# Strassen products of float32 replaced, from the second token block on, by three float32r passes over 12-bit operand parts

## Chip, core and metric

One core of one Trainium2 chip. The metric is the time of one execution of the program on the device in microseconds (us), from its own clock; lower is better. A profile of one execution is taken by the hardware profiler. Engines: PE (TensorE, matmul; PEld is its weight load), DVE (VectorE), ACT (ScalarE), POOL (GpSimd), SP (SyncE, which issues the DMAs here).

## The reference

Two parts, one after the other. First a retention recurrence over 4 x 8 heads, 768 steps and head size 64; then, on its output read as 3,072 tokens of 512 values, a two-layer network with an ELU between.

```python
for t in range(S):
    state = gamma[None, :, None, None] * state + np.einsum('bhd,bhe->bhde', k[:, :, t], v[:, :, t])
    y[:, :, t] = scale * np.einsum('bhd,bhde->bhe', q[:, :, t], state)
...
h = x @ w_in
g = np.where(h > 0.0, h, alpha * (np.exp(np.minimum(h, 0.0)) - 1.0))
return (g @ w_out).astype(np.float32)
```

x is 3,072 x 512, w_in 512 x 2,048, w_out 2,048 x 512, all float32. Both weight matrices reach the device as 64-bit floats and are decoded there.

## The kernel before

Tokens go in six blocks of 512. The retention of a block is worked in four chunks of 128 tokens: score products (L319) masked by DVE (L330), state products (L359) summed by DVE (L371), outputs (L415, L430) scaled by DVE into `xb` or `xt` (L405). It is cut into five steps (`retention_step`), which are put between the matmuls of the block before.

Block 0 is worked while the weights arrive. A weight piece (1,024 columns of 64-bit floats, 1 MB) is loaded into one of three `stage` tiles, prepared by three ACT instructions (L171, L173, L175) and decoded by two of DVE (L198, L201). Layer 1 of block 0 uses plain float32 matmuls (`plain_first`, L518 and L542), four of 512 columns for each of 16 groups of 128 hidden values. Layer 2 of block 0 (`second_of_first`, L632) is one level of Strassen: seven products in place of eight on quarters, with sums of the weight pieces (`sums_of_pieces`, L582) and of the hidden values (`inputs_of_first`, L561) made by DVE, and closing sums at L616.

From block 1 on: while block 0 runs its layer 2, DVE forms the combinations of weights that later Strassen levels need (`combine_w_out` L668, `combine_w_in` L695, `combine_small` L852), and SP stores them to scratch memory on the device. Block 1 has one level of Strassen in layer 1 (`first`, L765) and two levels in layer 2 (`second_twice`, L924). Blocks 2 and 3 are taken together, as are 4 and 5 (`NB` = 2 rounds): layer 1 has two levels for the products that can have them (`big_twice`, L1152) and one for the rest (`big_rest`, L1199); layer 2 has two levels, 7 x 7 products of four matmuls (`second_big`, L1248). A product ends in PSUM; ACT lifts it (L1163, L1256) or DVE adds it to another (L1167, L1260), and further DVE sums make the inputs of the next product (`quarters_of`, L894; `next_big_input`, L1230). ELU is two ACT instructions (L1214, L1215) and one of DVE (L1216).

The order of work on each engine is the order of the program text: nothing is rescheduled. Python generators are stepped by hand so that, for example, a retention step stands between two products. Every engine, and the queue of SP, works its instructions in that order, and an instruction that waits holds up all behind it on its engine. Weights for the later products come from scratch memory through a ring of tiles (`wq`): `want` lists them in order of use, and `fetch` (L830) issues a load when `done` has released a tile. The chunks of q, k and v (1 MB each, four tiles in `ldpool`) come through the same SP queue (L113), and so do the stores of results.

PSUM has eight banks: four in pool `ps_r` (retention, and some accumulators of block 0) and `a`, `a`, `b`, `d` in `ps_f`, handed out by `bank`.

Of the kernel before, what the change touches and what calls it, by code (L numbers as in the profile page):

```python
# [10 lines left out]
FP32 = mybir.dt.float32  # L11
I32 = mybir.dt.int32
# [3 lines left out]
ALU = mybir.AluOpType  # L16


@with_exitstack
def kernel(  # L20
# [4 lines left out]
    scratch: bass.AP,  # L25
    scratch2: bass.AP,
    scratch3: bass.AP,
    scratch4: bass.AP,
# [3 lines left out]

# [14 lines left out]
    NQ = 4  # L68
    NF = DFF // P // 2
# [9 lines left out]
    mpool = mid.enter_context(tc.tile_pool(name="mpool", bufs=4))  # L79
    hpool = mid.enter_context(tc.tile_pool(name="hpool", bufs=4))  # L80
    small = mid.enter_context(tc.tile_pool(name="small", bufs=6))
# [3 lines left out]

    early = ctx.enter_context(ExitStack())
    stage = early.enter_context(tc.tile_pool(name="stage", bufs=3, side="right"))
    t4 = early.enter_context(tc.tile_pool(name="t4", bufs=1, side="right"))
    so_ = t4.tile([P, 2, 7, 256], FP32, name="so")


    gnames = ["C11", "C12", "C21", "C22", "T3"]
    gq = {x: const.tile([P, DFF // P // 2, TH], FP32, name="g" + x) for x in gnames}
    gq["T1"] = gq["C12"]
    four = lambda x: gq[x].rearrange("p (i a) t -> p i (a t)", a=2)
    g_plain = [four(x)[:, i, :] for x in gnames[:4] for i in range(4)]

# [17 lines left out]
    def hold(t, other):  # L115
# [4 lines left out]

    w_all = const.tile([P, NQ, 14 * TH], FP32, name="w_all")
    w_a_, w_b_, w_x_ = (
        w_all[:, :, 1024 * g : 1024 * g + 1024].rearrange("p n (f c k d) -> p n f c k d", f=2, c=2, k=2) for g in range(3)
    )
    w_y_ = w_all[:, :, 3072:3584].rearrange("p n (f k d) -> p n f k d", f=2, k=2)
    w_a, w_b, w_x, w_y = ([x[:, n] for n in range(NQ)] for x in (w_a_, w_b_, w_x_, w_y_))
    s_of = lambda n: (w_y[n], w_x[n][:, :, 0], w_x[n][:, :, 1])
    NPIECE = 2 * NQ + NF  # L130
# [20 lines left out]

    def prepare(parts=1, by_vector=False, between=None):
# [5 lines left out]
        if n < 2 * NQ:  # L160
            dst = (w_a, w_b)[n % 2][n // 2].rearrange("p a b c d -> p (a b c d)")
        else:

            dst = w_x[n % NQ].rearrange("p a b c d -> p (a b c d)")
        todo = []
        for part in range(parts):
            if part and between:
                between()
            c = slice(part * 1024 // parts, (part + 1) * 1024 // parts)
            lo, hi, flat = t[:, c, 0], t[:, c, 1], dst.bitcast(U32)[:, c]  # L170
            nc.scalar.activation(flat, lo, AF.Copy, scale=2.0**-29)  # L171
            top = dst.bitcast(F8).rearrange("p (c b) -> p c b", b=4)[:, c, 3]
            nc.scalar.activation(top, hi.bitcast(FP32), AF.Copy, scale=2.0**-120, saturate=False)  # L173
            if not by_vector:
                nc.scalar.activation(lo.bitcast(FP32), hi.bitcast(FP32), AF.Copy, scale=2.0**-112)  # L175
            todo.append((lo, flat, hi if by_vector else None))
        prepared.append((dst, todo))


    ORDER_F = [f for n in range(NF // 2) for f in (n, NF // 2 + n)]  # L180


    quarters = lambda f: scratch.rearrange("(s k) p (f c) -> k f p s c", k=2, f=4)[f // 4, f % 4]

    used = lambda f, a, b: slice(a, b, 2 if f < NF // 2 else 1)

    def decode(fine=False):
# [7 lines left out]
        for c, flat, hi in todo:  # L195
            if hi is not None:
                vec.tensor_scalar(c.bitcast(FP32), hi.bitcast(FP32), 2.0**-112, None, ALU.mult)
            vec.tensor_scalar(c, c, 3, 0x7FFFFFF8, ALU.logical_shift_left, ALU.bitwise_and)  # L198
            if fine:
                yield  # L200
            vec.tensor_tensor(out=flat, in0=c, in1=flat, op=ALU.add)  # L201
            yield
        load_piece()
        if n >= 2 * NQ:
            f = ORDER_F[n - 2 * NQ]
            nc.sync.dma_start(quarters(f)[:, used(f, 2, 8)], dst.rearrange("p (s c) -> p s c", c=P)[:, used(f, 2, 8)])
# [4 lines left out]

# [23 lines left out]
    nc.vector.tensor_scalar(vf, vf, scale, None, ALU.mult)  # L237
# [36 lines left out]

    xb = const.tile([P, 4, TB], FP32, name="xb")
    xt_ = const.tile([P, 4, 2, TH], FP32, name="xt")
    xt = [xt_[:, n] for n in range(4)]

    x_of = lambda tb: xb if tb in (0, 3, 5) else xt_.rearrange("p j a t -> p j (a t)")

    xt1 = [xb[:, n].rearrange("p (a t) -> p a t", a=2) for n in (1, 2, 3, 0)]
# [15 lines left out]
    def state(tb, n):  # L299
# [3 lines left out]
        if (tb, n) == (0, 3):  # L303

            return xt[0].rearrange("p a t -> p (a t)")[:, 0:256].rearrange("p (h e) -> p h e", e=D)
# [168 lines left out]
    def combine_x_parts(tb=None):  # L474
        sub = lambda o, x, y: nc.vector.tensor_tensor(out=o, in0=x, in1=y, op=ALU.subtract)
        b11, b12, b21, b22 = (x_of(tb)[:, 2 * r : 2 * r + 2, half[t]] for r in range(2) for t in range(2))
        t1, t2, t3, t4_ = xt1 if tb == 1 else xt
        sub(t1, b12, b11)
        yield
        sub(t2, b22, t1)  # L480
        yield
        sub(t3, b22, b12)
        yield
        sub(t4_, b21, t2)

# [7 lines left out]
    def elu(g, h, depth=1, then=None):  # L493


        r = epool.tile([P, 512], FP32, name="r", tag="r", bufs=3)
        e = r if len(h.shape) == 2 else r.rearrange("p (a c) -> p a c", c=P)
# [3 lines left out]
        def last():  # L501
            nc.vector.scalar_tensor_tensor(g, e, -1.0, h, ALU.add, ALU.max)
            if then:
                then()
# [5 lines left out]
    def plain_first():  # L510

        tiles = [(n, w, row, fi) for n in range(NQ) for w, row in ((w_a, 0), (w_b, 1)) for fi in range(2)]
        banks = []

        def part(k, columns):
            n, w, row, fi = tiles[k]
            for j in range(4):
                nc.tensor.matmul(  # L518
                    banks[k][:, columns], lhsT=w[n][:, fi, j // 2, j % 2, :], rhs=xb[:, j, columns],
# [14 lines left out]
        for k in range(5):  # L534
            part(k, half[1])
            n, w, row, fi = tiles[k]
            elu(g_plain[row * NF + 2 * n + fi], banks[k])
            yield
        for k, (n, w, row, fi) in enumerate(tiles[5:]):
            hp = bank("aabd"[k % 4]).rearrange("p a b -> p (a b)")  # L540
            for j in range(4):
                nc.tensor.matmul(  # L542
                    hp, lhsT=w[n][:, fi, j // 2, j % 2, :], rhs=xb[:, j, :], start=(j == 0), stop=(j == 3)
                )
            elu(g_plain[row * NF + 2 * n + fi], hp)
# [3 lines left out]
    def of_first(r, f, t, count=2):  # L549

        i = (r * NF + f) % 4
        g = gq[gnames[(r * NF + f) // 4]]
# [23 lines left out]
    def sums_of_pieces(n):  # L576
# [3 lines left out]
        both = w_all[:, n % NQ : n % NQ + 2, 2048:3072]  # L580
# [15 lines left out]
        for x in range(2):  # L596
            f = ORDER_F[n + x]
            of = sums[n + x].rearrange("p a (d c) -> p (a d) c", c=P)
            nc.sync.dma_start(quarters(f)[:, used(f, 8, 16)], of[:, used(f, 0, 8)])

    def small_of_pieces(at):

        sources = [
            (decoded[2 * NQ + n].rearrange("p r (d c) -> p (r d) c", d=2)[:, 1:4], sums[n])
            for n in (2 * at, 2 * at + 1)
        ]
        return combine_w_out(at, *sources)

    def second_of_first():
# [8 lines left out]
        def store(k):  # L618
            nc.sync.dma_start(out[0, k // 2, k % 2].rearrange("p d c -> p (d c)"), out_t[k].rearrange("p a b -> p (a b)"))

        for n, f in enumerate(ORDER_F):
            wo, so, x = decoded[2 * NQ + n], sums[n], inputs[f]
            a21, a11, a12, a22 = (wo[:, r, 256 * d : 256 * d + 256] for r in range(2) for d in range(2))
            w = {1: a11, 2: a12, 3: so[:, 0], 4: a22, 5: so[:, 1], 6: so[:, 2], 7: so[:, 3]}
            at_end = n == NF - 1
            if at_end:
                m1, u2, v, u3 = (mpool.tile([P, 2, TH], FP32, name="m", tag="m") for _ in range(4))
# [29 lines left out]


    SEVEN = {1: 0, 2: 1, 4: 2, 3: 3, 5: 4, 6: 5, 7: 6}
    to_send = []  # L660

    def send_small():
        while to_send:
# [1225 lines left out]
```

## Time and profile before

| | |
|---|---|
| runs | 620.98, 623.10 (median), 625.47 us |
| profiled execution: span of its instructions | 621.4 us |
| PE's first matmul, and end of its last | 1.5 us, about 618.4 us |
| block 0 ends, block 1's first product starts | 134.75 us |
| PE, DVE, ACT, POOL busy | 611.4, 496.7, 261.0, 21.2 us |
| DMA moved | 125.14 MB, 201 GB/s mean |
| granted PE clock | 1.000 throughout |

No own time of the profiled execution stands beside its span; the first instruction to the last is what the page measures, and the median of the three runs is 1.7 us more. Reading the page: a group's row gives the engine, the operation, `out<-in` by tile names, the shape, the count, then its busy time and the mean of one in nanoseconds, then the idle time of the engine before them and who ended it. Matmul ends are modelled, so the distance between starts is the better measure of a matmul. One float32 matmul leaves two records in the trace.

### The profile page before, as it was taken

To read this page: it belongs to the slowest core of one execution; us is meant where nothing else is said; L and a number is where in the kernel's file an instruction comes from. 1 tells how busy PE (TensorE), PEld (TensorE's weight loads), DVE (VectorE), ACT (ScalarE), POOL (GpSimd) and SP (SyncE) were. 2 spreads that over 40 slices of the span, in tenths; PEclk is the share of its full clock that TensorE was granted. 3 is DMA by queue.
4 is the path that set the end of the run, shared out by engine and by line. 5 is a ranking of instruction groups with operands and counts; after the bars stand their busy time and mean duration, and the time that the engine had idled before them with its cause. 6 is when DMAs were issued, how large, how long until landed. Compare 5 with 4: busy or idle time off the path is not lost.

```text
span 621.4 us, 13415 instructions
## 1 busy us (share of the span) xinstructions
PE 611.4 (98%) x5446; PEld 480.9 (77%) x5446; DVE 496.7 (80%) x776; ACT 261.0 (42%) x446; POOL 21.2 (3%) x30
## 2 busy tenths in 40 slices
PE   8999999999999999999999999999999999999998
PEld 6764568888889998888545888888888744788886
DVE  5768889989889875677888987898546897888885
ACT  5888844205542111236898210100144798511110
POOL 2011000000000001000010000110000000000000
PEclk9999999999999999999999999999999999999999
DMA  8697569789575898786811445873654523356453
GB/s 295 285 374 303 174 205 269 235 242 274 204 234 151 301 374 310 231 250 199 274 49 67 122 134 154 268 275 108 206 159 143 151 69 93 118 148 187 153 150 117
DMA packets 79278, 125.14 MB, mean 201 GB/s; under 512 B 6128, under 2 KB 46832, under 8 KB 74480
## 3 DMA queue, kind: packets, MB, share of 16 engines
q1 hardware_dynamic: 79216, 124.28, 62.1%
q8 instruction: 43, 0.70, 0.4%
q14 instruction: 19, 0.16, 0.1%
HBM read 94.63 MB, written 29.62 MB: 200 GB/s over the span
## 4 chain that ended last, share of the span: by engine, by line
PE 86%; DVE 4%; DMA 3%; ACT 3%; issue 2%; SPq 0%; DVEq 0%
PE pa L1248 15%; PE pa L1152 9%; PE pd L1248 8%; PE pa L1199 6%; PE pd L1152 4%; PE pa L765 4%; PE pd L1199 4%; PE pb L1248 4%; PE x L632 3%; DMA wq<-scratch_dram 2%; PE pa L924 2%; PE pa L542 2%; PE pb L1152 2%; PE pa L632 2%; PE pb L1199 2%; PE y L415 2%
## 5 line engine op out<-in xcount | busy, mean ns | idle before, releaser
L1256 ACT COPY ms<-pa 128x256 f32<-128x256 f32 x41 | 15.3, 372 | 108.5 <-PE pa L1248 105.5
L1248 PE MATMUL pa<-gC,wq 128*128 128x256 f32 x224 | 53.1, 381 | 0.0
L1248 PEld LDWEIGHTS pa<-gC,wq 128*128 128x128 f32 x224 | 42.1, 190 | 6.8 <-DVE gT L1216 0.5
L1215 ACT ACTIVATE r<-r 128x512 f32<-128x512 f32 x64 | 40.3, 630 | 2.0
L1163 ACT COPY m<-pa 128x512 f32<-128x512 f32 x32 | 18.7, 585 | 48.9 <-PE pa L1152 48.8
L293 POOL TENSOR_TENSOR chunk<-chunk,vf 128x512 f32<-128x512 f32 x16 | 18.0, 1124 | 381.3 <-DMA chunk<-in_qkv_dram 201.1
L1260 DVE TENSOR_TENSOR res<-pd,ms 128x256 f32<-128x256 f32 x26 | 11.0, 422 | 25.0 <-PE pd L1248 14.1
L1152 PE MATMUL pa<-ts,wq 128*128 128x256 f32 x104 | 26.9, 384 | 0.0
L1248 PE MATMUL pa<-ts,wq 128*128 128x256 f32 x112 | 26.8, 382 | 0.0
L1248 PE MATMUL pd<-w_all,wq 128*128 128x256 f32 x112 | 26.6, 380 | 0.1
L171 ACT ACTIVATE w_all<-wraw 128x1024 uint32<-128x1024 uint32 (+1 forms) x19 | 19.2, 1008 | 16.9 <-PE x L632 9.0
L1248 PE MATMUL pd<-ts,wq 128*128 128x256 f32 x104 | 24.7, 380 | 0.2 <-DVE ts L894 0.2
L1230 DVE TENSOR_TENSOR gC<-w_all,gC 128x1024 f32<-128x1024 f32 x20 | 24.2, 1260 | 0.0
L1248 PEld LDWEIGHTS pd<-w_all,wq 128*128 128x128 f32 x112 | 21.2, 190 | 3.4 <-DVE w_all L894 0.6
L1248 PEld LDWEIGHTS pa<-ts,wq 128*128 128x128 f32 x112 | 21.0, 190 | 2.9
L1248 PE MATMUL pa<-w_all,wq 128*128 128x256 f32 x96 | 22.9, 381 | 0.0
L173 ACT ACTIVATE w_all<-wraw 128x1024 fp8e4<-128x1024 f32 (+1 forms) x19 | 22.6, 1189 | 0.6
L1152 PEld LDWEIGHTS pa<-ts,wq 128*128 128x128 f32 x104 | 19.3, 190 | 4.5 <-ACT m L1163 0.8
L1216 DVE SCALAR_TENSOR_TENSOR w_all<-r,w_all 128x512 f32<-128x512 f32 x32 | 22.0, 688 | 0.7 <-ACT r L1215 0.6
L1248 PEld LDWEIGHTS pd<-ts,wq 128*128 128x128 f32 x104 | 19.7, 190 | 3.2 <-DVE ts L894 0.6
L1199 PE MATMUL pa<-ts,wq 128*128 128x512 f32 x48 | 22.1, 592 | 0.0
L1199 PE MATMUL pa<-gC,w_all 128*128 128x512 f32 x48 | 22.1, 592 | 0.0
(327 smaller groups left out, 1458.0 us busy)
## 6 DMA issues: line engine op xcount, KB each, us to landing
wq<-scratch_dram SPq DMA_DIRECT2D x191, 256.0 KB, 3.2
chunk<-in_qkv_dram SPq DMA_DIRECT2D x22, 1024.0 KB, 7.6
wraw<-in_w_dram SPq DMA_DIRECT2D x15, 1024.0 KB, 7.1
out_dram<-res SPq DMA_DIRECT2D x7, 512.0 KB, 3.3
scratch_dram<-gT SPq DMA_DIRECT2D x12, 256.0 KB, 4.3
wq<-scratch_dram SPq DMA_DIRECT2D x24, 128.0 KB, 3.1
scratch_dram<-w_all SPq DMA_DIRECT2D x12, 256.0 KB, 3.4
scratch_dram<-w_all SPq DMA_DIRECT2D x24, 128.0 KB, 3.2
```

Of the source, the lines that this page charges most:

```text
L171: nc.scalar.activation(flat, lo, AF.Copy, scale=2.0**-29)
L173: nc.scalar.activation(top, hi.bitcast(FP32), AF.Copy, scale=2.0**-120, saturate=False)
L293: eng.tensor_tensor(out=v, in0=v, in1=vf[:, i].unsqueeze(2).to_broadcast([C, H, D]), op=ALU.mult)
L632: nc.tensor.matmul(X[j][:, d, :], lhsT=w[j][:, d * P : d * P + P], rhs=x[j], start=(n == 0 and d == 0), stop=at_end, skip_group_check=True,)
L765: nc.tensor.matmul(ps[:, fi, :], lhsT=w[:, fi, j2, :], rhs=x[:, j2, :], start=(begin and fi == 0 and j2 == 0), stop=(j2 == 1), skip_group_ ...
L1152: nc.tensor.matmul(ps[:, f, :], lhsT=w[:, f, :], rhs=big_xs[j][k], start=(begin and f == 0), stop=True, skip_group_check=True,)
L1163: nc.scalar.copy(o, ps)
L1199: nc.tensor.matmul(ps, lhsT=w[:, k, :], rhs=layer_x[j][:, k], start=False, stop=(k == 1), skip_group_check=True,)
L1215: nc.scalar.activation(r, r, AF.Exp, scale=-1.0)
L1216: return lambda: nc.vector.scalar_tensor_tensor(g, r, -1.0, g, ALU.add, ALU.max)
L1230: nc.vector.tensor_tensor(out=quarter(to, r, t), in0=quarter(x, r, t), in1=quarter(y, r, t), op=op)
L1248: nc.tensor.matmul(ps, lhsT=w[:, f, :], rhs=ts[j][k][:, f // 2, f % 2, :], start=(begin and f == 0), stop=(f == 3), skip_group_check=True,)
```

## The change

Block 0 keeps its products. From block 1 on there is no Strassen: each float32 operand is cut into a high part and a low part of 12 bits, of type float32r, and a product is made of three passes accumulated in PSUM: high x high and low x low, then the bank is multiplied by 1 + 2^-12 (`scaled`), then a third pass with the differences of the parts on both sides. Five blocks of 512 tokens follow, each with 16 groups of 12 passes in layer 1 and 16 groups of 12 passes in layer 2, all with 512 columns.

- Weights of layer 2: `parts_of_w_out` cuts each decoded piece into three parts (one ACT copy, two DVE instructions of 1,024 columns) in one tile, and stores them to scratch in three DMAs of 512 KB. It is called eight times, from the 13th step of layer 1 of block 0 to the end of its layer 2.
- Weights of layer 1: `parts_of_w_in` cuts each of 16 tiles (ACT copy, DVE low part, POOL difference) and stores high and low part; the first two are made at the end of block 0, the others inside layer 1 of block 1. In later blocks high and low come back by DMA, and POOL makes the difference (`third_of_w_in`).
- Activations: `split_x` cuts the input of a block, `split_g` each of 16 groups of hidden values (ACT copy, DVE low part, difference by DVE or, for odd groups, POOL).
- The high part of w_out stays on chip (`wo1`); its low part and difference are loaded again for each block, through a ring of eight tiles.
- Retention of the next block now stands inside layer 1 of each block, the chunk loads (`load`) and `scale_v` of the block after that inside layer 2.
- All combinations of weights, inputs and products of the later Strassen levels go, with their scratch memory.

The core of the diff (removed: `combine_x_parts`, `combine_w_out`, `combine_w_in`, `strassen`, `first`, `second_twice`, `big_twice`, `big_rest`, `second_big` and what they call):

```diff
+    def stt(o, a, by, b, op):
+        nc.vector.scalar_tensor_tensor(o, a, by, b, ALU.mult, op)
+
+    def parts_of_w_out(n):
+        t = w_parts.tile([P, 3, 2, DM], F32R, name="wp", tag="wp")
+        piece, (hi, lo, d) = flat(w_x_[:, n % NQ]), (flat(t[:, x]) for x in range(3))
+        nc.scalar.activation(hi, piece, AF.Copy, scale=W_PART * CUT)
+        stt(lo, piece, W_PART, hi, ALU.subtract)
+        stt(d, hi, R, lo, ALU.subtract)
+        f = ORDER_F[n]
+        for x in range(3):
+            nc.sync.dma_start(s_out[x, f : f + NP + 1 : NP].rearrange("f p c -> p f c"), t[:, x].bitcast(FP32))
...
+    def split_g(tb, f, by_pool=False):
...
+        nc.scalar.activation(g_hi[f], g, AF.Copy, scale=R * CUT)
+        stt(g_lo[f], g_hi[f], -1.0 / R, g, ALU.add)
+        (nc.gpsimd if by_pool else nc.vector).tensor_tensor(out=g_d[f], in0=g_lo[f], in1=g_hi[f], op=ALU.subtract)
...
+    def split_x(tb, i):
+        x, (hi, lo, d) = x_of(tb)[:, 2 * i : 2 * i + 2], (xp[:, n, 2 * i : 2 * i + 2] for n in range(3))
+        nc.scalar.activation(hi, x, AF.Copy, scale=CUT * PART / X_DOWN)
+        stt(lo, x, PART / X_DOWN, hi, ALU.subtract)
+        stt(d, hi, R, lo, ALU.subtract)
...
+    def fetch(count=1):
+        for _ in range(count):
+            if wanted:
+                name, source = wanted.popleft()
+                got[name] = ring.tile([P, TB], F32R, name="w", tag="w")
+                nc.sync.dma_start(got[name].bitcast(FP32), source)
...
+    def parts_of_w_in(f, tiles):
+        hi, lo, d = got[1, 0, f], got[1, 1, f], got[1, 2, f] = tiles
+        w = w_of(f).rearrange("p k c -> p (k c)")
+        nc.scalar.activation(hi, w, AF.Copy, scale=R * CUT)
+        stt(lo, hi, -1.0 / R, w, ALU.add)
+        nc.gpsimd.tensor_tensor(out=d, in0=lo, in1=hi, op=ALU.subtract)
+        for n, t in enumerate((hi, lo)):
+            nc.sync.dma_start(s_in[n, f], t.bitcast(FP32))
...
+    def first_two(tb, f):
+        hp = flat(ps_r.tile([P, 2, TH], FP32, name="hp", tag="r") if f < 2 else bank("aabd"[(f - 2) % 4]))
+        banks1[f] = hp
+        for n in range(2):
+            for k in range(NK):
+                one_pass(hp, got[tb, n, f][:, k * P : k * P + P], xp[:, n, k], start=(n == 0 and k == 0))
+        scaled(hp, tb == 1 and f % 2 == 1)
+
+    def first_third(tb, f):
+        for k in range(NK):
+            one_pass(banks1[f], got[tb, 2, f][:, k * P : k * P + P], xp[:, 2, k], stop=(k == NK - 1))
...
+    def second_two(tb, acc, f, ds=range(4)):
+        for d in ds:
+            for n, x in enumerate((g_hi, g_lo)):
+                w = got[tb, 3, f] if n else wo1[:, f]
+                one_pass(acc[d], w[:, columns(f, d)], x[f], start=(f == 0 and n == 0))
...
+        elif n == 5:
+            run(parts)
+            early.close()
+            xp = ctx.enter_context(tc.tile_pool(name="xp", bufs=1, side="right")).tile([P, 3, NK, TB], F32R, name="xp")
+            parts_of_w_out(5)
+            parts_of_w_out(6)
         elif n == 6:
+            parts_of_w_out(7)
+            split_x(1, 0)
+            split_x(1, 1)
+            first_parts.close()
...
+            for f in range(2):
+                parts_of_w_in(f, [ahead_.tile([P, TB], F32R, name=f"ahead{f}{x}") for x in range(3)])
+
+    first_two(1, 0)
+    first_two(1, 1)
+    first_third(1, 0)
+    first_third(1, 1)
...
+    for tb in range(1, NTB):
+        last, done = tb + 1 == NTB, 0
+        for f in range(2 if tb == 1 else 0, NF):
+            first_two(tb, f)
+            if f and (tb, f) != (1, 2):
+                first_third(tb, f - 1)
+                first_end(tb, f - 1)
+            if tb > 1:
+                fetch(2)
+                third_of_w_in(tb, f + 2)
+            elif f + 2 < NF:
+                parts_of_w_in(f + 2, ring_tiles())
...
+            if tb == 1:
+                if f < 4:
+                    for n in (0, 1):
+                        load(2 * CPB + 2 * (f - 2) + n)
+                elif f < 8:
+                    scale_v(2 * CPB + f - 4)
+                if f >= 2 and f < 14:
+                    for n in range(4 * (f - 2) // 3, 4 * (f - 1) // 3):
+                        nc.sync.dma_start(wo1[:, n].bitcast(FP32), s_out[0, n])
+            if f in ((6, 8, 10, 12, 13) if tb == 1 else (3, 5, 7, 9, 11)):
+                retention_step(tb + 1, (6, 8, 10, 12, 13).index(f) if tb == 1 else f // 2 - 1)
+            if tb > 1 and f in (10, 12, 14):
+                split_g(tb, done)
+                done += 1
...
+        second_layer(tb, acc, done, between, beside)
+        for n, _ in enumerate(end_of_second(tb, acc)):
+            if n < 2 and not last:
+                split_x(tb + 1, n)
+            if n in (6, 8) and not last:
+                third_of_w_in(tb + 1, (n - 6) // 2)
```

`second_layer` runs `second_two` for f = 0 to 15, with one `fetch` after each and each `split_g` two f ahead; loads of the next chunks stand at f = 3 to 6 and `scale_v` at f = 10 to 13. `end_of_second` scales the four banks, runs the third passes of all f, copies each bank out (ACT and DVE in turn) and stores it.

## The prediction

> **What bounds the kernel now.** First the page: engines, the chain that ended last, the rows that price the new work, the DMA rows.
>
> ```profile
> span 621.4 us, 13415 instructions
> ...
> PE 611.4 (98%) x5446; PEld 480.9 (77%) x5446; DVE 496.7 (80%) x776; ACT 261.0 (42%) x446; POOL 21.2 (3%) x30
> ...
> PE 86%; DVE 4%; DMA 3%; ACT 3%; issue 2%; SPq 0%; DVEq 0%
> ...
> L1230 DVE TENSOR_TENSOR gC<-w_all,gC 128x1024 f32<-128x1024 f32 x20 | 24.2, 1260 | 0.0
> ...
> chunk<-in_qkv_dram SPq DMA_DIRECT2D x22, 1024.0 KB, 7.6
> ...
> out_dram<-res SPq DMA_DIRECT2D x7, 512.0 KB, 3.3
> ...
> scratch_dram<-so SPq DMA_DIRECT2D x4, 512.0 KB, 4.9
> ```
>
> PE works through the whole span and carries 86% of the chain; DVE at 80% runs beside it. So a saving must come out of the PE stream, and a cost is anything that makes PE wait. Next, PE's timeline at three places; columns are start, length, line, operands, records.
>
> ```profile
> 128.71 1.89 PE L632 MATMUL x<-gC,w_all 128*128 128x256 f32 x8
> 130.44 1.03 PE L632 MATMUL pa<-h,so 128*128 128x256 f32 x4
> ...
> 134.75 1.89 PE L765 MATMUL pa<-xt,w_all 128*128 128x256 f32 x8
> ```
> ```profile
> 194.23 1.06 PE L924 MATMUL pa<-gC,wq 128*128 128x128 f32 x8
> 195.12 1.06 PE L924 MATMUL pb<-gC,wq 128*128 128x128 f32 x8
> ```
> ```profile
> 301.69 3.60 PE L1199 MATMUL pa<-gC,w_all 128*128 128x512 f32 x8
> 305.12 1.45 PE L1199 MATMUL pb<-gC,w_all 128*128 128x512 f32 x3
> ```
>
> Start to start counts, since ends are modelled. One f32 matmul leaves two records. A record takes 0.216 us at 256 columns (1.73 / 8), 0.111 at 128 (0.89 / 8) and 0.429 at 512 (3.43 / 8). Block 1 begins at 134.75. Then POOL against DVE, from their timelines at one moment:
>
> ```profile
> 208.22 1.07 POOL L293 TENSOR_TENSOR chunk<-chunk,vf 128x512 f32<-128x512 f32 x1 [154.60 <-PE pa L924]
> ```
> ```profile
> 207.69 0.69 DVE L936 TENSOR_TENSOR res<-res 128x512 f32<-128x512 f32 x1
> 208.30 1.53 DVE L894 TENSOR_TENSOR ts<-gT 128x512 f32<-128x512 f32 x1
> 209.87 0.69 DVE L894 TENSOR_TENSOR ts<-gT,ts 128x512 f32<-128x512 f32 x1
> ```
>
> A DVE instruction with both inputs in SBUF that meets a POOL one goes from 0.69 to 1.53: they take turns. Last, ACT at the last weight piece to be decoded: it waits for PE.
>
> ```profile
> 108.97 1.16 ACT L171 ACTIVATE w_all<-wraw 128x1024 uint32<-128x1024 uint32 x1 [4.07 <-PE x L632]
> 110.16 1.39 ACT L173 ACTIVATE w_all<-wraw 128x1024 fp8e4<-128x1024 f32 x1
> 111.41 1.15 ACT L175 ACTIVATE wraw<-wraw 128x1024 f32<-128x1024 f32 x1
> ```
>
> **The change part by part.**
>
> *PE stream.* From 134.75 on, before: 728 matmuls of 256 columns (112 of L765, 224 of L1152, 392 of L1248) at 0.431, 96 of 512 (L1199) at 0.86, 196 of 128 (L924) at 0.222: 314 + 83 + 43 = 440 us. After: five blocks, two layers, 16 x 12 passes: 1,920 float32r passes of 512 columns. The trace holds no such pass. Lower bound: a quarter of an f32 matmul of 512 columns, 0.216, since f32 here costs twice two streams of its columns and a pass over 12-bit parts is one of the four part-products. Upper bound: one whole f32 record, 0.429. I take 0.2157, the nearest to "one stream": 414 us, so -26; the upper end is a rival below. Each pass loads its weights as each record does now; records of 128 columns keep a pitch of 0.111 with a load each, so loads hide.
>
> *Retention* of blocks 2 to 5 has the same instructions, about 9.2 us per block (37 in all), before and after: 0.
>
> *Handover at the end of block 0.* The Strassen sums of w_in and w_out (L668, L695, L852) go. Added are eight parts_of_w_out: one ACT copy of 1,024 columns (1.15, L175), two dependent DVE instructions of 1,024 with two SBUF inputs (1.24, L1230), three stores of 512 KB (3.3 to 4.9 to land; I take 3.5). Their tile has one buffer, so the next copy waits for all three stores: a period of 7.2. Queue order settles the rest. On ACT, part 4 stands behind the piece shown above, which ends at 112.6. On DVE, behind part 3 (done at 107.5) stand decode 1.9, sums 2.1, inputs 2.9, 0.6, decode 1.9 (as now at 101 to 113), so part 4's DVE work starts at 116.9 and its stores land at 123; part 5 stands behind 7.6 more and starts at 127.0, landing at 133; parts 6 and 7 follow at 7.2: DVE done at 144, landed at 147.5. Then split_x (four DVE of 1.22, to 148.9) and the first w_in parts, whose memory those stores release. PE, done with block 0 at about 137 (2.3 late, since the inputs of piece pair 2 come at 114.5, not 110.3), starts block 1 at 148.5. Next it waits for scaled(1), behind seven closing sums of block 0 on DVE (155.8), and for block 0's output stores, whose memory the third w_in tiles reuse (157.4). It reaches f = 4 at 162.8, having done 9.5 us of work since 134.9: +18. Bounds: 12, if the new DVE instructions cost 0.69 as the one-input ones of 1,024 (L198) do, 12 of them counting; 24, with stores at 4.9. Idle of 11 us has no row: PE's longest wait now is 1.5 and the granted clock 1.000. The Trainium skill (TensorE: Matmul & The Clock Gate, Part 1) says that an idle window of about 3.4 us halves the clock until a busy one has passed; by that the sum would be up to 1.7 higher, an estimate.
>
> *Block 1, layer 1.* SP issues the four 1 MB chunks of block 2 at 163 to 166 among stores of w_in parts and loads of wo1. The 5.0 MB up to the last chunk need 14 us at 356 GB/s (what 220 to 240 us moves with DMA fully busy), landing at 178; PE comes to block 2's scores at 171.6: +6.5 (0 if PE itself comes late, 9 if the stores go first). Per f, PE has twelve passes, 2.59; ACT has a part's copy 0.63, relu 0.59, exp 0.63 and half a scaled() 0.3, 2.2 in all; DVE a part 0.69, elu 0.69, half a scaled() 0.35 and a sixteenth of the retention's 9.5, 2.3. Both stay under PE, without much room: were DVE the longer one, each 0.1 per f would cost 1.6.
>
> *Block 1, layer 2 start.* Block 1 has no split made ahead. After PE's last third pass of layer 1 stand relu, exp and a copy on ACT (1.9) and then five dependent DVE instructions of 0.69 before the third low part, 5.5 in all; PE has 1.9 of work until it needs that part: +3.6 (2 to 4.5). Later blocks make three splits ahead.
>
> *POOL.* It gets some 115 new instructions of 1.04 to 1.12. In layer 2, two f need three DVE instructions of 0.69 and one POOL of 1.04 in turns: 3.1 us under PE's 3.45. Four scale_v in blocks 1 to 3 eat that margin: +1 each; each layer 2 starts 0.3 late: together +4.5 (0 to 13).
>
> *At nothing.* SP issues 64 tile loads, 4 chunk loads and 4 stores per later block at 0.33 to 0.43 each (rows of SP now), some 28 of 92 us; a load waits for the PE that frees its tile, and output stores stand ahead of the next block's third and fourth weight tiles, which still have 3 us. scaled() in PSUM (0.59 ACT) under the next twelve passes; elu as now; weight tiles: at worst 16 x 256 KB in 13.8 us, 304 GB/s, where the trace holds 336 to 356. If that cover goes, each tile late costs up to 0.8.
>
> *End and edges.* Copy 0.7 and store 2.2 after the last pass: +0.4. The old stretch is 483.5 long, 440 + 37 explained; I let half of its 6.5 us of edges go: -3.
>
> Sum on the span: 621.4 - 26.4 + 18 + 6.5 + 3.6 + 4.5 + 0.4 - 3 = 625. The median of the runs, 623.1, stands 1.7 above that span: 626.7.
>
> **The rivals.**
>
> *Handover hidden (faster).* If the period of a part is about 5 and not 7.2, parts 5 to 7 end near 137 and PE goes on at once: -11 of the 18, and the chunks' wait shrinks by some 3: 613. For it: the DVE price is borrowed, and 512 KB has landed in 3.3. Against: one buffer, two dependent 1.24s. It decides once PE starts block 1 before 140.
>
> *Layer 2 bound by DVE and POOL in turn (slower).* With 0.15 for each of five hand-offs a pair of f takes 3.85, not 3.45: 0.4 x 6.5 pairs x 5 blocks = +13: 640. It decides where the pair passes 3.45. For it: 1.53 above. Against: three tiles of lead.
>
> *A pass streams at half rate (much slower).* A record now reads 128 x 256 x 4 B in 0.216 us, 608 GB/s; a float32r pass at 0.216 reads twice that. If 608 is the port's limit, a pass takes 0.429: +410: 1037. Against: that f32 also splits operands may be what sets the record. The Trainium skill (SBUF — State Buffer, A bandwidth-pool intuition that's wrong) gives about 614 GB/s for PE's moving operand, for bf16; the row agrees, and neither shows float32r.
>
> **How the numbers follow.** The sum above 0.48 (617 to 636), hidden handover 0.30 (600 to 617), layer 2 bound 0.16 (633 to 655), half rate 0.06. One per cent, about what a measurement here can tell from no change, is 617 to 629: of the sum's 0.48, 0.27 lies within, 0.20 above, 0.01 below. So faster 0.31, same 0.27, slower 0.42. 604 to 644 leaves out the half rate, 0.06 of the hidden handover and 0.06 of the bound layer.
>
> **What would show it.** Passes 0.216 apart; block 1's first pass near 148; a PE wait on chunk DMA near 172; 94 us per later block. Passes at 0.43, or no PE gap at the handover, would make it wrong.

## The result, and the profile after

The changed kernel takes **663.3 us** (median of 4 runs, 661.8 to 664.5) against 622.9 us for the kernel before on the same chip (4 runs): a ratio of 1.0653, 95% interval 1.0619 to 1.0686. Predicted were 626.7 us, 0.6% above the kernel before, with a range of 604 to 644 and slower (0.42) as the likeliest of three cases. The kernel is slower, but the time lies above the range. The profiled run took 661.8 us, its span 659.9, 38.5 more than the span before.

The same lines of the page as before, of the changed kernel:

```profile
span 659.9 us, 13444 instructions
...
PE 621.1 (94%) x5326; PEld 488.3 (74%) x5326; DVE 358.3 (54%) x527; ACT 306.4 (46%) x467; POOL 182.1 (28%) x149
...
PEclk9999999979799999999999999999999999999999
...
PE 77%; DVE 9%; DMA 7%; ACT 4%; issue 2%; POOL 0%; SPq 0%; DVEq 0%; ACTq 0%; POOLq 0%
```

DVE has lost 138 us of work and POOL won 161, and neither is near its limit. PE is still the engine that carries the chain, but its share of the chain fell from 86% to 77%, and two slices near the start of block 1 show a digit of 7 for the granted clock, where it had been 9 (90% or more) throughout. What PE waited for, longest first (after the colon: total us, times, longest us):

```profile
PE hp L673 <- ACT ahead L658: 8.5, 1, 8.5
PE pa L673 <- DVE w_in L467: 6.4, 4, 1.6
PE sc L295 <- DMA chunk<-in_qkv_dram: 5.6, 2, 4.2
PE pd L673 <- DVE w_in L467: 2.6, 4, 0.7
PE pb L673 <- ACT gh L617: 1.9, 1, 1.9
PE pa L673 <- DVE g L467: 1.6, 1, 1.6
```

The handover (8.5), the chunks (5.6) and block 1's layer 2 (1.9 + 1.6) were in the sum. The second and fourth lines were not: 9.0 us in four blocks, at the start of layer 2, where an accumulator takes over a PSUM bank that the ELU of layer 1's last groups still reads. The handover at the start of block 1, in PE's timeline (start, length, operands, records; in brackets the idle time before and who ended it):

```profile
144.07 7.11 PE L673 MATMUL hp<-xp,ahead 128*128 128x512 f32 x20 [8.54 <-ACT ahead L658]
158.90 2.03 PE L673 MATMUL pb<-xp,w 128*128 128x512 f32 x8
```

The first row is block 1's first pass, the second its group 4. Where was the predicted gain of 26 us in the PE stream? PE's timeline, first in layer 1 (moving operand xp, then the next group), then in layer 2 (moving operand gd):

```profile
261.81 4.84 PE L673 MATMUL hp<-xp,w 128*128 128x512 f32 x20
266.48 2.03 PE L673 MATMUL pa<-xp,w 128*128 128x512 f32 x8
```
```profile
248.94 1.98 PE L673 MATMUL pa<-gd,w 128*128 128x512 f32 x8
250.76 0.39 PE L673 MATMUL pb<-gd,w 128*128 128x512 f32 x1
```

Start to start: 4.67 / 20 = 0.2335 us a pass in layer 1, 1.82 / 8 = 0.2275 in layer 2 (over longer stretches of the trace 0.2333 and 0.2267, with hardly a deviation in layer 2). The sum had 0.2157. Over 960 passes in each layer that is 224.0 + 217.6 = 441.6 us, and 440 was there before: the saving of 26 us is gone, entirely, before any wait is counted.

And three stretches of the span at and after such waits (columns: stretch, length, busy time and count of PE, of weight loads, of VectorE, ScalarE and POOL, then the granted clock, the DMA share and GB/s):

```profile
132.00:152.00 20.00, 11.01 (x39) 8.37 (x38) 14.90 (x18) 5.15 (x7) 2.90 (x2) 0.74 0.67 247
170.00:182.00 12.00, 7.83 (x82) 6.40 (x83) 4.21 (x7) 1.04 (x2) 2.31 (x2) 0.72 0.94 371
208.00:222.00 14.00, 10.30 (x36) 7.41 (x35) 8.42 (x14) 5.66 (x11) 0.35 (x1) 0.88 0.59 201
```

If the clock is either full or half, a mean of 0.74 over 20 us is 2 x 0.26 x 20 = 10.4 us at half speed, then 6.7 and 3.4 us. The three lie at the handover, at the chunks and at block 1's layer 2. The last began at 213.7 us, behind the wait of 1.9 us (211.2 to 213.1) and ahead of the one of 1.6 us (219.6 to 221.2), after which the clock stayed full.

The terms of the prediction against the profile, in us of the span:

| term | predicted | measured | how measured |
|---|---|---|---|
| PE stream | -26.4 | +1.6 | 441.6 - 440 |
| handover | +18 | +10.9 | waits 8.5 + 0.5 + 1.3; block 0 done 0.6 later |
| half clock | 0 (estimate beside the sum: 1.7) | +6.5 | a little under half of the three stretches without the idle time in them: 2.3 + 2.6 + 1.6 |
| chunks of block 2 | +6.5 | +5.6 | wait of sc |
| block 1, layer 2 start | +3.6 | +3.5 | 1.9 + 1.6 |
| POOL and DVE in turns | +4.5 | 0 | one PE wait of 0.2 for gl, none for gd |
| banks at later layer 2 starts | not in the sum | +9.0 | 6.4 + 2.6 |
| end and edges | -2.6 | +1.4 | the rest of 38.5 |

### The profile page after: what moved, and what is told of

Read it like the earlier page. It is cut to its first block, busy times and chain, and to the rows that moved or that the text cites. A ratio compares the mean times of both kernels' runs of the same rounds, so it can differ in the third digit from the quotient of the medians.

```text
span 659.9 us, 13444 instructions
## 1 busy us (share of the span) xinstructions
PE 621.1 (94%) x5326; PEld 488.3 (74%) x5326; DVE 358.3 (54%) x527; ACT 306.4 (46%) x467; POOL 182.1 (28%) x149
## 4 chain that ended last, share of the span: by engine, by line
PE 77%; DVE 9%; DMA 7%; ACT 4%; issue 2%; POOL 0%; SPq 0%; DVEq 0%; ACTq 0%; POOLq 0%
PE pa L673 31%; PE pd L673 15%; PE pb L673 14%; DMA scratch_out_dram<-wp 3%; DMA chunk<-in_qkv_dram 3%; DVE wp L182 3%; PE hp L673 3%; PE pa L505 3%; PE y L391 2%; PE sc L295 2%; PE kv L335 2%; PE y L406 1%; ACT r L463 1%; PE pa L481 1%; PE pd L505 1%
## 5 line engine op out<-in xcount | busy, mean ns | idle before, releaser
L670 POOL TENSOR_TENSOR w<-w 128x512 fp32r<-128x512 f32 x64 | 84.3, 1318 | 166.6 <-DMA w<-scratch_in_dram 72.9
L673 PE MATMUL pa<-xp,w 128*128 128x512 f32 x480 | 124.2, 401 | 1.5 <-ACT w L658 1.3
L673 PEld LDWEIGHTS pa<-xp,w 128*128 128x128 f32 x480 | 90.3, 190 | 24.3 <-ACT w L658 1.8
L182 DVE SCALAR_TENSOR_TENSOR gl<-gh,w_in 128x512 fp32r<-128x512 f32 x64 | 55.4, 870 | 54.3 <-ACT gh L617 54.2
L619 POOL TENSOR_TENSOR gd<-gl,gh 128x512 fp32r<-128x512 f32 x35 | 47.2, 1349 | 116.2 <-DVE gl L182 116.2
L673 PE MATMUL pa<-gh,wo 128*128 128x512 f32 x160 | 62.8, 393 | 8.0 <-DVE w_in L467 6.4
L673 PE MATMUL pa<-gl,w 128*128 128x512 f32 x160 | 62.4, 390 | 0.0
L673 PE MATMUL pb<-xp,w 128*128 128x512 f32 x180 | 47.8, 400 | 0.0
L673 PE MATMUL pd<-xp,w 128*128 128x512 f32 x180 | 47.1, 396 | 0.0
L467 DVE SCALAR_TENSOR_TENSOR w_in<-r,pa 128x512 f32<-128x512 f32 x32 | 21.9, 684 | 42.9 <-ACT r L464 42.9
L673 PE MATMUL pa<-gd,w 128*128 128x512 f32 x160 | 44.4, 389 | 0.0
```

Source lines behind the costliest of these rows:

```text
L182: nc.vector.scalar_tensor_tensor(o, a, by, b, ALU.mult, op)
L619: (nc.gpsimd if by_pool else nc.vector).tensor_tensor(out=g_d[f], in0=g_lo[f], in1=g_hi[f], op=ALU.subtract)
L670: nc.gpsimd.tensor_tensor(out=got[tb, 2, f], in0=got[tb, 1, f], in1=got[tb, 0, f], op=ALU.subtract)
L673: nc.tensor.matmul(ps, lhsT=w, rhs=x, start=start, stop=stop, skip_group_check=True)
```

## The experiments

**Theories.** Main theory: a float32r pass has a price of its own beyond its columns, 13 to 20 ns (11 to 18 above 0.2157 us), and this is what took the gain. Rivals for the pass: the price is per column (four bytes at one column a step); it is the weight load; it is adding into a bank; it is the order or the place of the operands. For the rest: the waits are single causes that can be removed one by one, against waits that only replace each other. A "clock" in the expectations is 1 / 2.4 of a nanosecond, the step between 256 and 512 columns below.

**Halves.** In `one_pass`:

```
+        for c in (slice(0, TH), slice(TH, TB)):
-        nc.tensor.matmul(ps, lhsT=w, rhs=x, ...
+            nc.tensor.matmul(ps[:, c], lhsT=w, rhs=x[:, c], ...
```

> Each 512-column float32r pass is issued as two passes of 256 columns with the same weights; nothing is left out. In the changed kernel a pass lies 0.2267 us from the next in layer 2 and 0.2333 us in layer 1. Theory A (a fixed cost of 13 to 20 ns in every pass, beside 512 columns at 0.417 ns): a pair takes 0.240 to 0.253 us and the time rises by 26 to 32 us, to about 690-695 us. Theory B (each column of four bytes costs 0.443 to 0.456 ns): a pair takes 0.227 to 0.233 us and the time stays within 3 us of 663 us. Theory C (the pitch is a weight load and its hand-over, whatever the columns): every half takes 0.227 us and the time rises by about 430 us.

Measured 680.2 us (one run). Layer 2 in its trace:

```profile
252.95 2.08 PE L674 MATMUL pa<-gd,w 128*128 128x256 f32 x16
254.87 0.40 PE L674 MATMUL pb<-gd,w 128*128 128x256 f32 x2
```

1.92 / 16 = 0.1200 us for 256 columns; 0.2267 for 512. So a column costs (226.7 - 120.0) / 256 = 0.417 ns, and 226.7 - 512 x 0.417 = **13.3 ns are a fixed price of each pass**, on the line through these two points. Theory A, at the lower end of its 13 to 20 ns; B and C fall: the extra does not grow with the columns, and the weight load does not set the pitch, as a pass of 0.120 us hides one too. (The rise is 17 us rather than 26 to 32, as layer 1's halves also come at about 0.121, without layer 1's surcharge.)

**Two bytes.** The passes read the upper half of each word: `a.bitcast(BF16)...[:, :, 1]` for both operands.

> The passes read the upper halves of the same float32 words as bfloat16 (every second two-byte element, so same addresses and same count of columns); the lower 16 bits of every operand part are left out of the products, all else stays. If the float32r type sets the pitch (as operand width or as its own kind of weight load), passes come at 0.213 to 0.216 us in both layers and the time falls by about 25 us, to about 637 us. If a 512-column pass costs 0.227 to 0.233 us for any type, the pitch and the 663 us stay.

Measured 652.2 us (one run). Layer 1 fell to about 0.227 us, layer 2 only to 0.226. Neither forecast came whole: layer 1 lost its extra, and both layers kept the rest of the price. But the elements were still 4 bytes apart. Hence the next one.

**Dense two bytes.** As above, but `g_hi`, `g_lo` and `g_d` are stored as adjacent bfloat16 (`.bitcast(BF16)[:, 0:TB]`); the low bits are left out of the products in both.

> As the kernel two_bytes (products of bfloat16, so the low bits are left out), but layer 2's moving operands are stored as adjacent bfloat16 values, so a pass reads 1 KB a partition in place of every second pair of bytes of 2 KB; weights and layer 1 stay as in two_bytes, where layer 2 took 0.2256 us a pass. If the width or the stride of what the pass reads sets the gap over 512 columns at 0.4167 ns = 0.2133 us, layer 2 falls to about 0.2133-0.2157 us and the time by 960 x 10 to 12 ns, about 10 us under two_bytes. If every pass of 512 columns has that gap, whatever it reads, layer 2 stays at 0.2256 us.

Measured 644.1 us (one run), 8 under two_bytes. Layer 2 of two_bytes, then of this kernel:

```profile
248.00 1.96 PE L674 MATMUL pa<-gd,w 128*128 128x512 bf16 x8
249.81 0.39 PE L674 MATMUL pb<-gd,w 128*128 128x512 bf16 x1
```
```profile
249.24 1.89 PE L675 MATMUL pa<-gd,w 128*128 128x512 bf16 x8
250.97 0.38 PE L675 MATMUL pb<-gd,w 128*128 128x512 bf16 x1
```

1.81 / 8 = 0.226 against 1.73 / 8 = 0.216 (0.2158 over 26 passes). Same type, weights and counts: the price hangs on a moving operand whose elements lie 4 bytes apart. (That the elements lie apart and that a pass spans twice the bytes come together here; no run separates the two.) Where a column takes twice 0.417 ns it does not show. The f32 record that the prediction borrowed is such a case, 0.2157 us or 518 clocks for 256 columns. A float32r pass at half clock is another: five of them, from 214.41 to 216.54 us of the changed kernel's trace, take 0.426 us each, and 512 columns at 2 x 0.417 ns are 0.427. The Trainium skill (TensorE: Matmul & The Clock Gate, "Wait — 56ns, not 53.3ns?") gives columns / 2.4 GHz plus about 2.5 ns, 215.7 ns at 512: the dense two-byte passes agree with 215.8, the float32r passes do not with 226.7, and there the measurement decides. The Trainium skill (SBUF — State Buffer, "A bandwidth-pool intuition that's wrong") gives about 614 GB/s for PE's moving operand; 128 x 512 x 4 bytes in 0.2267 us are 1,156 GB/s, so that is no ceiling here.

**Layer 1's extra 6.7 ns: adding, banks, order.** Three kernels: `start=True` in every pass, which leaves out the sums over passes; the third product's passes put between the next group's; rows taken as hi, lo of row 0, hi, lo of row 1 and so on, third product in the order 0, 2, 1, 3.

> Every float32r pass starts its bank afresh instead of adding to it: the sums over passes are left out, all else stays. If adding to a bank that the pass before also wrote sets the pitch of 0.2333 us in layer 1 against 0.2267 us in layer 2, layer 1 falls to 0.2267 us or below and the time falls by at least 6 us; if adding explains all of it, both fall to 0.2133-0.2157 us and the time by about 27 us. If adding has no price, nothing moves.

> In layer 1 the four passes of the third product of one group are issued in turn with the last four passes of the next group, which write another bank; nothing is left out. If a run of passes into one bank is what makes layer 1 slower than layer 2, the eight passes in turn come at 0.2267 us and the first four, all in one bank, at 0.2333 us: 0.2289 us over a group of 12, about 4 us less in all, unless the third product then waits for the scaling of its bank (one ACT operation of 0.58 us), which would give it back. If it is the operand of layer 1, wherever it writes, all 12 stay at 0.2333 us.

> In layer 1 the passes go row by row, high and low part in turn (8 KB apart), and the third product takes rows 0, 2, 1, 3, so that no pass reads the 2 KB right behind those of the pass before; same passes, same memory layout, another order. In the changed kernel layer 1's passes read adjacent rows one after another and come at 0.2333 us; layer 2 mostly jumps and comes at 0.2267 us. Theory of the adjacent row: layer 1 falls to 0.2267 us and the time by about 6 us to 657 us. Rival (where the tile lies, or layer 1 itself): nothing beyond 2 us.

Measured 661.5, 667.4 and 663.2 us (the last a ratio of 1.0642, 1.0616 to 1.0668), and in all three layer 1 stayed at 0.2333-0.2337. Adding, runs into one bank and adjacent rows are out. Of the 4 us that banks_in_turn is longer, 1.4 lie in block 0, which its edit does not touch (it ends at 136.9 us, not 135.5, after 3.4 us at half clock from 11.5); the rest was not followed up.

**Layer 1's extra: the place of the operand.** The tile of x's parts is allocated a little longer, which moves its start; in left_off_64 all tiles of the left side, weights among them, move by 32 bytes instead:

```
-....tile([P, 3, NK, TB], F32R, name="xp")
+....tile([P, 3 * NK * TB + 8], F32R, name="xp")     # operand_at_64; 280: like_g; 216: at_256
+    const.tile([P, 8], FP32, name="pad")            # left_off_64
```

> The tile with the parts of x, layer 1's moving operand, is allocated 32 bytes longer, which moves its start in every partition from 172000 (2687 x 64 + 32 bytes) to 171968 (2687 x 64); the operands of layer 2 start on multiples of 64 already. Nothing else changes. If the start of the operand off a 64-byte boundary is the price of 16 clocks that separates layer 1 (0.2333 us a pass) from layer 2 (0.2267 us), layer 1 falls to 0.2267 us and the time by 960 x 6.7 ns = 6.4 us, to about 657 us. If it is something else in layer 1 (traffic of the ELU, the tile's far end of the memory), nothing moves beyond 2 us.

> The three parts of x get a start each: the high part on a multiple of 128 bytes, the low part 32 bytes past a multiple of 64 (as it was), the third on a multiple of 2048. By the theory of the start, of each group of 12 passes the four with the high part and the four with the third come at 0.2267 us and the four with the low part at 0.2333 us; the third shows whether a start on a larger power of two takes anything off the 32 clocks that remain. If the start has no price, all twelve are at 0.2333 us.

> One 32-byte tile ahead of all others moves every tile of the left side by 32 bytes: the parts of g and all weights then start 32 bytes past a multiple of 64, as the parts of x do already. If a moving operand's start off 64 bytes costs 16 clocks a pass, layer 2 rises from 0.2267 to 0.2333 us, layer 1 stays, and the time rises by 6 us. If what counts is how the moving operand lies against the weights, layer 1 falls to 0.2267 us and layer 2 stays. If the start has no part in it, neither moves.

> The parts of x start at 896 bytes past a multiple of 2048 in each partition, just as those of g do (before: 2016 past). If the place within 2 KB decides, layer 1 comes at 0.2267 us and 6 us are gained on the 663 us; if a start on 64 bytes gives half and layer 1's own traffic the rest, about 0.2295 us as in operand_at_64 and 3 to 4 us; if neither, 0.2333 us and nothing.

> The parts of x start 256 bytes further within 2 KB than the parts of g and the weights do (operand_like_g: 0 bytes, 0.2267 us for most passes; operand_at_64 and left_off_64: 1088 bytes, 0.2295 us; changed kernel: 1120 bytes, 0.2333 us). If the distance to the weights sets the price, layer 1 takes a value other than 0.2267 us, or even less; if any distance that is a multiple of 128 is as good, it is 0.2267 us as in operand_like_g.

The start of the same 20 passes and of the next group, in operand_at_64, left_off_64, operand_like_g and operand_at_256:

```profile
262.50 4.76 PE L673 MATMUL hp<-xp,w 128*128 128x512 f32 x20
267.10 2.00 PE L673 MATMUL pa<-xp,w 128*128 128x512 f32 x8
```
```profile
262.68 4.76 PE L674 MATMUL hp<-xp,w 128*128 128x512 f32 x20
267.27 2.09 PE L674 MATMUL pa<-xp,w 128*128 128x512 f32 x8
```
```profile
262.43 4.70 PE L673 MATMUL hp<-xp,w 128*128 128x512 f32 x20
266.96 2.12 PE L673 MATMUL pa<-xp,w 128*128 128x512 f32 x8
```
```profile
261.36 4.70 PE L673 MATMUL hp<-xp,w 128*128 128x512 f32 x20
265.89 2.00 PE L673 MATMUL pa<-xp,w 128*128 128x512 f32 x8
```

0.2300, 0.2295, 0.2265 and 0.2265 us. My theory of a 64-byte boundary fell with left_off_64: it put layer 2's operands off the boundary, and layer 2 stayed at 0.2267 while layer 1, which had not been moved, fell. What moved there is the left side, and of it these passes read only the weights. Distances between x's parts and the weights, by the starts of the tiles (the traces hold no addresses), modulo 128 bytes: 96 in the changed kernel (0.2333), 64 in the first two (0.2295-0.2300), 0 in the last two (0.2265). So **layer 1's extra goes with the place of the moving operand against the tiles of the left side**, most likely the weights; no run moved the weights alone. How exactly stays open: in three_places (663.6 us, one run) distances of 0, 96 and 0 in one kernel gave medians of 232, 234 and 232 ns for its three parts, where 227, 233 and 227 were expected, so a pass's price is not its own distance alone. And it needs 4-byte elements: two_bytes has the tiles of the changed kernel, and its layer 1 comes at 0.227 us, its layer 2 at 0.226. The pitch carries this finding, not the time: operand_like_g gave 660.0 us (ratio 1.0602, 1.0570 to 1.0635) and operand_at_64 660.9 (1.0637, 1.0584 to 1.0690), and both intervals overlap that of the changed kernel; left_off_64 and operand_at_256, one run each, 660.0 and 657.6.

**Banks.** From block 2 on, groups 14 and 15 go to the other pool's banks, and layer 2 begins with banks "aabd" in place of "bdaa".

```
-... if f < 2 else bank("aabd"[(f - 2) % 4]))
+... if f < 2 or (tb > 1 and f >= NF - 2) else bank("aabd"[(f - 2) % 4]))
-        acc = [flat(bank(x)) for x in "bdaa"]
+        acc = [flat(bank(x)) for x in ("bdaa" if tb == 1 else "aabd")]
```

> From block 2 on, the last two groups of layer 1 use banks of the other pool and layer 2's accumulators begin with the two banks whose ELU is longest done, so layer 2 never waits for the ELU of groups 13 to 15. The profile of the changed kernel has 2.25 us of such waits in each of blocks 2 to 5. If they are on the path, the time falls by 4 x 2.25 = 9 us, to about 654 us. If the split of the first values of layer 2 or the next block's groups take their place, under 4 us.

Measured 652.1 us, ratio 1.0489 (1.0459 to 1.0518): 0.0164 of 622 us, 10 us less. Both waits on L467 in blocks 2 to 5 are gone from its list. The 9.0 us were on the path.

**Handover and chunks.** In `handover`, w_out parts 1, 3 and 5 and the first w_in parts live in the chunk tiles, and part 7 comes after the w_in parts; in `chunks_early`, the loads of block 2 stand ahead of `first_two(1, 0)`.

> Three of the eight w_out parts and the first two w_in parts use the four chunk tiles, which stand empty then, so that a part no longer waits for the stores of the part before, and the parts of w_in come ahead of the last part of w_out. In the changed kernel TensorE waits 8.5 + 0.5 + 1.3 us there and runs at half clock until 148.9 us of the span, which costs its 20 passes about 2.4 us more. Theory (the single buffer of the parts is what delays the first pass): the 8.5 us fall below 3 us, the clock stays up, and the time falls by 7 to 11 us, to about 653-656 us. Rival (the splits themselves, on VectorE, or the stores' bandwidth set the start): the first pass still comes more than 5 us after the last product of block 0, and the time falls by under 4 us.

> The four loads of block 2's chunks are issued before layer 1 of block 1, about 12 us earlier in the queue, into tiles that stand empty. In the changed kernel TensorE waits 4.3 + 1.4 us for them near 173 us and then runs at half clock for some 6.8 us. Theory (the queue position is what makes them late): both waits and the slow stretch go, 5.6 us + about 2.7 us, to about 655 us. Rival (bandwidth: 4 MB that the stores and loads of the parts then wait behind): the wait moves to the parts of w_in or the output, and under 3 us are gained.

Handover: 655.9 us, ratio 1.0532 (1.0510 to 1.0554), 7.5 us less. Chunks: 660.6 us, 1.0593 (1.0563 to 1.0622), 3.7 us less, the interval just touching that of the changed kernel. What came in place, in the waits of handover, then in the waits and PE's timeline of chunks_early:

```profile
PE hp L678 <- DVE hp L682: 4.1, 1, 4.1
```
```profile
PE pa L673 <- ACT w L658: 4.7, 2, 3.0
168.45 2.14 PE L673 MATMUL pa<-xp,w 128*128 128x512 f32 x8 [2.96 <-ACT w L658]
```

In the first the 8.5 us are gone, and group 1's scaling, on VectorE behind block 0's output sums, is late next, with 6.8 us at half clock behind it, so the clock did not stay up as expected; in the second the chunk wait is gone, and 3.4 us of it came back as a wait for weight parts, whose transfers now stand behind 4 MB of chunks. The idle time of 2.96 us there brought no half clock: the eight passes behind it take about 2 us. So the theory held for the handover, and for the chunks its rival, bandwidth, was half right.

**All together.** `together` joins these (of block 2's chunk loads, two stand ahead of the last part of w_out and two at group 2), with group 1 scaled by ScalarE, the first splits of layer 2 ahead in block 1 too (`if f in (10, 12, 14)`), x's parts 32 bytes lower and block 2's retention one group later; `together_2` sums block 0's output into the tile of x, frees the banks in block 1 too and puts x's parts like g's; `together_3` loads the last two chunks earlier and moves the scores to group 8.

> All remedies at once: the parts in the chunk tiles, group 1 of block 1 scaled by ScalarE in place of VectorE (which is busy with block 0's output), two of the chunk loads ahead of the last part of w_out and the other two at group 2, block 2's retention one group later, layer 2's banks free, the first splits of layer 2 ahead in block 1 too, x's parts 32 bytes lower. If the gains add up (7.4 + 4 of the 4.1 us wait that was left + 6 to 8 for the chunks with the clock + 11 for the banks + 3.5 for the splits + 2.4 for the start), the time is 663.3 - 35 = about 628 us, still above the 623 us of before, since 1,920 passes at 0.2267-0.2296 us stay 23 us dearer than at 0.2157 us. If the waits replace one another, it stays above 640 us.

> As together, but block 0's output is summed into the tile of x, which stands empty, so the weights' first ring tiles no longer wait for its stores; layer 2's banks are freed in block 1 too, with its retention steps closer together; x's parts lie at the same place within 2 KB as the parts of g. If the 10.2 us wait was that store, it falls below 4 us, and with it the half clock (5.1 us), 2.9 us of waits at block 1's layer 2 and 1.5 us of pass price: about 635.6 - 15 = 620 us, level with or just under the 623 us of before. What then stays of the change is a pass of 0.2267 us: at 0.2157 us it would be 1,920 x 11 ns = 21 us less. If another wait takes the store's place (the sums of block 0 on VectorE, or the first split), 626 us or more.

> As together_2, with the last two chunk loads of block 2 issued ahead of group 2 of block 1 and the scores at group 8 in place of 7 (2.8 us later). If the 3.0 us wait is the landing of those chunks, it falls below 0.5 us and the half clock behind it goes too (3.4 us), less about 1 us of wait for the banks that the outputs free later: 624.2 - 5.4 = about 619 us, 0.6% under the 622.5 us of before. If it is something else, within 1.5 us of 624 us.

Measured 635.6 us (ratio 1.0207, 1.0172 to 1.0242), 624.2 us (1.0029, 1.0006 to 1.0051; 12 runs, 621.4 to 628.8) and 628.4 us (1.0116, 1.0085 to 1.0147); expected were 628, 620 and 619 if each remedy worked whole. The longest waits of together and of together_2:

```profile
PE pa L678 <- ACT w L663: 10.2, 1, 10.2
```
```profile
PE sc L300 <- issue: 3.6, 3, 3.0
PE pa L678 <- DVE w L182: 2.1, 1, 2.1
```

The 10.2 us were block 0's output stores, whose memory the first weight tiles reuse: with the output elsewhere 2.1 us are left. That version is level with the kernel before (0.3% above), not under it. Together_3 missed: the scores no longer wait for chunks beyond 1.5 us, but two new waits of 2.5 us (weight parts behind the chunks) and 2.2 us (banks that the outputs free late) came, and its ratio is 0.9% higher, some 5 us. So no version here beats the kernel before. In the profiled execution of together_2 (627.8 us) all waits after block 0 and its one half-clock stretch come to some 12 us (four of the twelve runs, of 621.4 to 625.0 us, had a clock of 1.000); the 1,920 passes at 0.2267-0.2279 us still cost 22 us more than at 0.2157.

## Why the prediction was wrong

The failed step is the first: *"I take 0.2157, the nearest to 'one stream'"*.

- **PE stream: the mis-sized term.** 0.2267 and 0.2333 us in place of 0.2157: 27 to 28 of the 35 us between the span of 625 that was predicted and 659.9. The bounds 0.216 to 0.429 held the value, but the lower one was taken as the price, because the row that it came from was the only one near it. That row is of a float32 matmul, whose two records take two clocks (of 0.417 ns) a column, and cannot show what 4-byte columns cost at one clock each. At 1,920 passes, 5 to 8% on one row is the whole gain; the range should have been opened upward by it. (The sum also enters 26.4 where its own terms, 440 - 414, give 26.) That slower was the likeliest case came out, but not for the reasons given: the forecast had PE gaining and the waits losing more.
- **Handover: mechanism right, size 7 us too large.** The first pass came at 144.1, not 148.5, and group 4 at 158.9, not 162.8, with 2.3 us of half clock in it that the table books apart. The period of a part was right (DVE began parts 5, 6 and 7 at 123.8, 131.0 and 137.7, so 7.2 and 6.7 apart), and so was the price of its DVE instructions (1.22); but DVE was done with part 3 at 104.5, not 107.5, and all later parts came 3 to 4 us earlier with it. The handover kernel, which gives three parts and the first w_in parts other memory and moves the last part back, let the first pass begin at 133.5: the named cause, the chain of parts behind one buffer, was the right one, though that kernel changes buffer and order together.
- **Half clock: underrated.** The idle times of 8.5 us, of 4.2 + 1.4 us and of 1.9 us each brought a stretch at half clock, 6.5 us in all; the estimate of 1.7 beside the sum counted one. The Trainium skill (TensorE: Matmul & The Clock Gate, Part 1) gives half the clock after an idle window of about 3.4 us. The lengths of the stretches, 10.2, 6.8 and 3.4 us, agree with such a window, but here an idle time of 1.9 us was enough, and the measurement decides.
- **Chunks (5.6 us for 6.5) and block 1's layer 2 (3.5 for 3.6): right.**
- **POOL and DVE in turns: the mechanism is there, its price is not.** The DVE splits average 870 and 897 ns against 0.69 us, POOL 1.32-1.35 us against 1.04-1.07, but PE waited 0.2 us for them in all. At the start of layer 2 stands a wait that the sum put at nothing ("elu as now"), the banks, for 9.0 us: the change reuses layer 1's last banks as accumulators, and the ELU of a group takes relu, exp and a DVE step before its bank is free. The banks_free kernel shows that they cost time: 10 us.
- **Rivals.** Handover hidden did not come (block 1 started at 144.1, not before 140); layer 2 bound by the turns did not; the half rate is refuted (0.2267, not 0.429). A later block takes 101 us (block 3 starts at 362.5, block 4 at 463.6), not 94: 5.5 us of pass price and 2.3 of banks.

## What to carry to other kernels

When a change is worth a few per cent of a stream of thousands of equal instructions, the price of that one instruction has to be measured, or its range carried at full weight to the total: a row of another form of it, even one that moves as many columns or takes about as long, is no price. Ask of each accumulator which late reader still holds its bank, and of each idle time of PE, from about 2 us on in these runs, what it may cost again in clock. A wait that is removed shows the next in its queue, so the gains of single remedies add only when memory, queue and bandwidth behind them are free as well.

## What the runs showed of the hardware

- A pass with a 4-byte moving operand at one column a clock: N x 0.417 ns + 13.3 ns for N columns (two points: 0.1200 us at 256, 0.2267 at 512); with adjacent 2-byte elements 0.2158 at 512, with 2-byte elements 4 bytes apart 0.226. At half clock the fixed price is not there (0.426 at 512). Why it is fixed and not per column stays open.
- The same pass takes 0.2265, 0.2295 or 0.2333 us with moving operand and weights 0, 64 or 96 bytes apart modulo 128, where all passes of a group have the same distance; with mixed distances (0, 96, 0) about 0.232 to 0.234.
- Stretches at half clock behind PE's idle times lasted 3.4, 6.8 or 10.2 us. Every idle time of 3.3 us and more brought one. Shorter ones did or did not: the same 1.9 us at the start of block 1's layer 2 did in eleven kernels and did not in four (two_bytes, dense_two_bytes, handover, chunks_early); 2.95 us did in together_2, 2.96 did not in chunks_early. The 1.6 us at the start of later layers 2 never did.
